# Attention with beacon keys and a gated FFN on one core: how the keys of the last three batches and the queries of the last batch are turned

## The chip, the cores and the metric

The kernel runs on one core of a Trainium2 chip, in one launch. The metric is the device time of one execution in microseconds. Before the change three runs took 399.99, 402.75 and 403.11 us, with a median of 402.75.

## The reference

Eight batches of eight heads attend, with 576 queries and 576 keys of width 64 per head, behind 16 beacon keys that every query sees; the rest is causal. The result goes through a gated FFN: 4608 tokens, width 512, hidden width 1536.

```
k_all = concatenate([beacon_k, k], axis=2)            # 16 + 576 = 592 keys
v_all = concatenate([beacon_v, v], axis=2)
scores = matmul(q, k_all.T) / sqrt(64)                # per batch and head
scores = where(key 16 + j is later than query i, -1e9, scores)
a = softmax(scores)
x = matmul(a, v_all)  -> (B * S, H * D) = (4608, 512)
out = (maximum(x @ w_gate, 0) * (x @ w_val)) @ w_out
```

## The kernel before, in words

The program is written out by a planner. Every piece of work is a `Task` with an engine, an estimated cost, the tasks that it needs and the buffers that it holds; `Plan.order` lets time run in the model, always takes the piece that can begin first (ties by priority), and the result is a fixed order of instructions for each engine. On the chip each engine goes through its order and waits on semaphores, so a cost that the planner has wrong turns into a wait and not into another order.

*Loading a batch* (`new_batch`, L497 to 676). Per batch there are a remainder each of keys and queries ("K", "Q"), four pairs of heads for keys and queries ("0" to "3", first the key pair, then the query pair) and five pieces of values. `load_pair` (L552) brings two heads of 512 tokens as float32 into a staging tile `st` (eight of them, L369). `rounded` (L508) casts it to bfloat16 in a tile `h16` (three, L371) on POOL, from batch 2 on. Then the pair is turned, so that the 64 features of two heads lie on the 128 partitions and the tokens along the columns of `kT` or `qT`:

- In batches 0 to 6 TensorE does it: `turned` (L522) issues four matmuls of the pair's four 128x128 blocks with the identity (L529) into one PSUM bank, and `evict` (L579) copies 128x512 on ScalarE or VectorE into `kT` or `qT`. The pair is loaded in runs of four tokens, 1 KB each (L563), so block j holds every fourth token, and `evict` puts the tokens in order again as it reads PSUM.
- In batch 7 (`TURN`) the DMA does it: the pair is loaded in two halves, in runs of one token of 256 bytes (L560), cast, and `dma_start_transpose` on the SP queue (L574) writes the four blocks straight to `kT` or `qT`, with no matmul and no eviction.

The remainder (64 tokens and 16 beacons of the keys, some 80 rows of the queries) goes through TensorE in all batches (`load_rest`, L610); for keys two copies bring it to `kT` (L635, L636).

*Scores* (`quad_scores`, L727). A quad is two pairs of heads, so there are two quads per batch. Each score matmul has 64 query columns as weights and up to 512 keys as the moving operand, and fills one 64x64 tile of the array; four of them (two pairs `i`, two heads `k`) go side by side. In batches 3 to 7 a quad has three steps (`STEPS2`, L337). The last holds "E", the last 64 queries against the first 512 keys, "e", the same against the next 64, and query tile 3 (256 keys):

```
for j, lo, n, b_, off in cols:        # L752
    for i in range(2):
        for k in ks:
            matmul(64x64 tile (k, i), columns off .. off + n, keys lo .. lo + n)
```

*Softmax* (`softmax`, L680). VectorE adds the mask and takes the row's lowest value in one instruction (L704, scores are negated), ScalarE writes the exponentials as bfloat16 to `pb` and their sum (L711), VectorE takes the reciprocal (L717), POOL scales (L722). From batch 1 on `pb` is transposed by DMA on the SP queue, 25 blocks of 128x128 in one instruction (L842); then TensorE makes the products with the values (L852) and the result is copied to `xT`. The last 16 queries of all heads are handled together per batch (`last`, L797, scores at L806).

*FFN* (`ffn`, L905). For ten spans of up to 512 tokens: gate and value matmuls (L913, L918), relu on ScalarE (L924), product on VectorE (L929), output matmuls (L944), eviction (L469 or L467 by the helper `copy`) and store from SP (L958). The FFN of earlier batches fills TensorE while later batches are in softmax. SP issues loads, transposes and stores in one order; loads, casts and scaling share POOL. In the first part of the plan, TensorE also runs matmuls on the identity that nothing uses (L996).

Of the kernel before, what the change touches and what calls it, by code (L numbers as in the profile page):

```python
# [35 lines left out]
TURN = (7,)  # L36
# [29 lines left out]
PACE = 38.0  # L66

# [229 lines left out]
def kernel(  # L297
# [42 lines left out]
    NB, NB0 = 25, 5  # L340

# [24 lines left out]
    kT_s = Slots(many(2, [P, NP, SK], BF16, "kT"))  # L366
# [121 lines left out]

    def heads(src, b, s0, sl):
        return src[b, :, s0:s0 + sl, :].rearrange("h s d -> s h d")  # L490
# [6 lines left out]
    def new_batch(b, prio, work):  # L497
        t = Batch()
        t.b = b
        steps = 2 * sum(len(x) for x in (STEPS2 if b > BIGSTEP else STEPS if b >= SPLIT else STEPS_AB + STEPS_CDE)) + 1  # L500
# [51 lines left out]
        def load_pair(kind, p, prio):  # L552

            src, s0 = {"k": (k, 0), "q": (q, 64 - Nb)}[kind]
            st = staged()

            def fetch(_):
                if b in TURN:
                    for i in range(2):
                        nc.sync.dma_start(st.tile.rearrange("p (n h d) -> p h n d", h=2, d=D)[:, i],  # L560
                                          src[b, 4 * (p // 2) + p % 2 + 2 * i, s0:s0 + MAIN, :].rearrange("(n p) d -> p n d", p=P))
                    return
                nc.sync.dma_start(st.tile.rearrange("p (h e) -> p h e", h=2),  # L563
                                  src[b, bass.ds(4 * (p // 2) + p % 2, 2, step=2), s0:s0 + MAIN, :].rearrange("h (p j) d -> p h (j d)", j=4))
# [3 lines left out]
            h16, ca = rounded(dst, st, P, neg_scale if kind == "q" else 1.0, prio, ld,  # L568
                              lambda to, src: [(to, src)] if b in TURN else [(
                to.rearrange("p (j h d) -> p h j d", h=2, j=4), src.rearrange("p (h j d) -> p h j d", h=2, j=4))])  # L570
            zeros = on_zeros.get(b) if kind == "q" else None
            c0 = Nb if kind == "k" else 64
            if b in TURN:
                t.rows[kind, p] = [add("DMA", (1.22, 0.177 * 4), lambda _: nc.sync.dma_start_transpose(  # L574
                    dst.tile[:, p, c0:c0 + MAIN].rearrange("p (j n) -> p j n", j=4), h16.tile), (ca, zeros), (h16, dst), prio[0] - TURN_FIRST)]
# [7 lines left out]
            t.rows[kind, p] = [add(("ACT", "DVE"), {"ACT": c_act(512), "DVE": c_dve(512)}, evict, (tu, zeros), (ps, dst), prio[1])]  # L583

# [25 lines left out]
        def load_rest(kind, prio):  # L610
# [21 lines left out]
            def evict(x):  # L632
                ps3 = ps.tile.rearrange("p (a n) -> p a n", a=NP)
                if kind == "k":
                    copy(x.engine, dst.tile[:, :, Nb + MAIN:], ps3[:, :, :REST])  # L635
# [27 lines left out]
        at, held = 0, None  # L663
# [16 lines left out]
    def softmax(t, parts, ph, prio, k):  # L680
# [3 lines left out]
        def view(i, lo=0):  # L684
            n, held, off = parts[i][:3]
            if len(held) == 1:
                return held[0].tile[:, off + lo:off + n]
            at = 512 * next(j for j, x in enumerate(bank) if x is held[0].tile)
            return psum[:, at + lo:at + n]
# [7 lines left out]
        for i, (n, held, _, msk, m, on, _, scored) in enumerate(parts):  # L697
            first = []
            if m < n:
                first = [add("DVE", c_max(n - m), lambda _, i=i, n=n, m=m: nc.vector.tensor_reduce(  # L700
                    out=at(7), in_=view(i)[:, :n - m], axis=AX.X, op=ALU.min), (scored,), held, prio + 0.001 * i + 0.0005 * k, 0.25)]

            def lowest(_, i=i, n=n, m=m, msk=msk):
                nc.vector.tensor_tensor_reduce(out=view(i, n - m), in0=view(i, n - m), in1=msk, scale=1.0,  # L704
                                               scalar=at(7) if m < n else 3.0e38,
                                               op0=ALU.add, op1=ALU.min, accum_out=at(i))

            lows.append(add("DVE", c_max(m), lowest, (scored, on, *first), held, prio + 0.001 * i + 0.0005 * k, 0.25))
        for i, (n, held, _, _, _, _, a, _) in enumerate(parts):
            def exp(_, i=i, n=n, a=a):  # L710
                nc.scalar.activation(ph.tile.rearrange("p a n -> p (a n)")[:, a:a + n], view(i), AF.Exp,  # L711
                                     bias=at(i), scale=-1.0, accum_out=at(4 + i))
# [14 lines left out]
    def quad_scores(t, g, step, phs, vals, prio, after):  # L727
# [23 lines left out]
        def scores(_):  # L751
            for j, lo, n, b_, off in cols:  # L752
                for i in range(2):
                    for k in ks:
                        r = slice(64 * k, 64 * k + 64)
                        nc.tensor.matmul(banks[k][b_].tile[64 * i:64 * i + 64, off:off + n],  # L756
                                         t.q.tile[r, 2 * g + i, 64 * j:64 * j + 64],
                                         t.kT.tile[r, 2 * g + i, lo:lo + n], start=True, stop=True)
# [17 lines left out]
    def quad(t, g, vals, prio, after):  # L776
# [4 lines left out]
        if PEQ(t.b, g):  # L781
            todo = list(range(NB_AB)) if ab else [i for i in range(21) if i not in (3, 7)] if t.b < SPLIT else list(range(NB))
            on_pe = [todo[i:i + 8] for i in range(0, len(todo), 8)]
# [13 lines left out]
    def last(t, prio):  # L797
# [17 lines left out]
    def finish(t, p, vals, ph, pt_s, blocks, on_pe, outs, prio):  # L815

        pt = Hold(pt_s, len(vals) + max(1, len(on_pe)))
        if on_pe:
            tr = []
            for todo in on_pe:  # L820
                tp = Hold(first_ps if t.b == 0 else v_ps, 2)
                z = len(todo)
                runs = []
# [4 lines left out]

                def turn(_, todo=todo, tp=tp):
# [4 lines left out]
                def evict(x, runs=runs, tp=tp):  # L834
                    for i, a, n in runs:
                        copy(x.engine, pt.tile[:, a:a + n, :].rearrange("p a n -> p (a n)"), tp.tile.bitcast(BF16)[:, i * P:(i + n) * P])

                u = add("PE", 0.06 * z, turn, outs + [on_ident], (ph, tp), prio - 4)
                more = 0.07 * (len(runs) - 1)
                tr.append(add(("ACT", "DVE"), {"ACT": c_act(z * P) + more, "DVE": 0.08 + 0.0006 * z * P + more}, evict, (u,), (tp, pt), prio - 4))  # L840
# [132 lines left out]
    for b in range(B):  # L973
        batches.append(new_batch(b, {0: -20, 1: RANK1}.get(b, b * T0 - 8), b * T0 - AHEAD if b else -20))
    for b in range(B):
        for i, vals in enumerate([("AB", "CDE")] if b >= SPLIT else [("AB",), ("CDE",)]):
            for g in range(2):
                quad(batches[b], g, vals, b * T0 + (4 * g if b >= SPLIT else 4 * i + 2 * g) - (AB_FIRST if b < SPLIT and i == 0 else 0), AFTER[b][i] if b < SPLIT else PACE * (b + g / 2))
        last(batches[b], b * T0 + 8)
# [50 lines left out]
```

## Time and profile before

| what | value |
|---|---|
| runs | 399.99, 402.75, 403.11 us, median 402.75 |
| profiled execution, its own time | 399.48 us |
| its span, first to last instruction | 397.8 us |
| mean granted TensorE clock | 0.998 |
| matmul 64 x 512 of the scores (L756), its own bar | 392 ns, 128 of them |
| relu of 128 x 512 (L924) | 604 ns |
| transposes of `pb` by DMA, issue to landing | 6.4 us median, 28 of them |

A row of instructions gives the line, the engine, the operation, output and input, the shapes and the count; behind the bar stand the busy time and the mean duration in ns, then the idle time of the engine just before and what ended it. PE is TensorE's matmuls and PEld its weight loads, DVE is VectorE, ACT ScalarE, POOL GpSimd; SPq is the queue of SyncE from which DMAs are issued, and the time of such a row is that of the issue. A matmul's bar is longer than its share of the queue, because matmuls are pipelined: what counts is the distance between starts.

### The profile page before, as it was taken

The page shows a single profiled execution, that of the slowest core. Times are in us where ns is not written, and L with a number is a line of the kernel's source. Part 1 is how long each engine was busy: PE and PEld are TensorE (multiplying, and loading weights), DVE is VectorE, ACT ScalarE, POOL GpSimd, SP SyncE. Part 2 cuts the span into 40 slices and gives each one's busy share as a digit, 9 for nine tenths or more (in the row PEclk, how much of TensorE's full clock was granted, in tenths as well). Part 3 has the DMA queues.
Part 4 walks back from the last instruction along what each step waited for, and adds up shares of the span by engine and source line. Part 5 has one row for each costly group of instructions (what it writes and reads, how often), then busy time and mean ns, then how long its engine had stood idle before and what let it go on. Part 6 is the DMA issues. An engine that isn't in the chain of part 4 may idle for free.

```text
span 397.8 us, 9897 instructions
## 1 busy us (share of the span) xinstructions
PE 386.6 (97%) x3235; PEld 203.8 (51%) x3278; DVE 287.6 (72%) x1024; ACT 261.7 (66%) x820; POOL 234.2 (59%) x454
## 2 busy tenths in 40 slices
PE   6999999999999999999999999999999999999995
PEld 4667855655454545455455445444454544444543
DVE  3999899788988697879697969687758733342432
ACT  2999699868967788668877878587737721320320
POOL 6899979849977576869669848646653520000000
PEclk9999999999999999999999999999999999999999
DMA  7999989999999799989999989798979184001102
GB/s 183 233 205 226 250 154 180 214 232 256 247 209 204 197 224 221 176 227 263 189 166 298 208 146 183 164 221 184 196 138 234 25 127 145 2 0 57 50 1 93
DMA packets 184100, 68.87 MB, mean 173 GB/s; under 512 B 158384, under 2 KB 179504, under 8 KB 184048
## 3 DMA queue, kind: packets, MB, share of 16 engines
q1 hardware_dynamic: 179216, 63.46, 73.7%
q0 software_dynamic: 4752, 4.72, 7.5%
q8 instruction: 25, 0.41, 0.5%
q14 instruction: 27, 0.22, 0.2%
q10 hardware_dynamic: 80, 0.07, 0.1%
HBM read 38.54 MB, written 9.44 MB: 121 GB/s over the span
## 4 chain that ended last, share of the span: by engine, by line
PE 88%; POOL 3%; DVE 3%; DMA 2%; issue 1%; SPq 1%; ACT 0%; POOLq 0%; ACTq 0%
PE f L918 23%; PE f L944 23%; PE f L913 22%; PE f L756 7%; PE f L852 6%; PE f L529 3%; DMA st<-in_q_dram 2%; POOL xT L722 2%; DVE f L704 2%; PE f L832 1%; PE f L996 1%; PE f L875 1%; PE f L806 1%; DVE osb L469 1%; POOL h L518 1%
## 5 line engine op out<-in xcount | busy, mean ns | idle before, releaser
L722 POOL TENSOR_SCALAR pb<-pb,small 128x448 bf16<-128x448 bf16 (+8 forms) x272 | 141.5, 539 | 70.5 <-DVE small L717 69.8
L711 ACT ACTIVATE pb<-f,small 128x320 bf16<-128x320 f32 (+8 forms) x272 | 143.9, 553 | 22.6 <-DVE small L704 17.7
L704 DVE CUSTOM_DVE_ANT_0 f<-f,mask 128x576 f32<-128x576 f32 (+8 forms) x288 | 133.7, 515 | 14.3 <-PE f L756 9.1
L918 PE MATMUL f<-xT,wv_r 128*128 128x512 bf16 (+3 forms) x467 | 107.3, 358 | 0.7
L913 PE MATMUL f<-xT,wg_r 128*128 128x512 bf16 (+3 forms) x468 | 105.4, 357 | 0.6
L929 DVE TENSOR_TENSOR hT<-g,f 128x512 bf16<-128x512 f32 (+3 forms) x120 | 75.4, 631 | 37.3 <-PE f L918 32.1
L944 PE MATMUL f<-wo_r,hT 128*128 128x512 bf16 (+3 forms) x438 | 99.6, 374 | 1.3 <-issue 0.5
L924 ACT ACTIVATE g<-f 128x512 f32<-128x512 f32 (+3 forms) x120 | 66.3, 562 | 50.9 <-PE f L913 44.2
L913 PEld LDWEIGHTS <-wg_r 128*128 128x128 bf16 x480 | 45.3, 98 | 43.7 <-issue 1.2
L918 PEld LDWEIGHTS <-wv_r 128*128 128x128 bf16 x480 | 43.4, 98 | 44.5 <-issue 5.2
L944 PEld LDWEIGHTS <-hT 128*128 128x128 bf16 (+2 forms) x456 | 42.1, 100 | 46.3 <-issue 2.1
L711 ACT ACTIVATION_READ_ACCUMULATOR pb<-f,small 128x1 f32 x272 | 60.9, 224 | 0.0
L518 POOL TENSOR_SCALAR h<-st 128x512 bf16<-128x512 f32 (+1 forms) x93 | 49.0, 541 | 11.0 <-DMA st<-in_q_dram 6.9
L469 DVE COPY osb<-f 128x512 f32<-128x512 f32 (+2 forms) x32 | 21.7, 682 | 28.1 <-PE f L944 27.7
L704 DVE DVE_READ_ACCUMULATOR2_ANT small<- 128x1 f32 x296 | 41.6, 141 | 0.0
L467 ACT CAST xT<-f 128x240 bf16<-128x240 f32 (+2 forms) x56 | 21.2, 385 | 30.7 <-PE f L852 29.5
L756 PE MATMUL f<-kT,qT 64*64 64x512 bf16 (+7 forms) x640 | 34.4, 295 | 0.1
L717 DVE RECIPROCAL small<-small 128x1 f32<-128x1 f32 (+3 forms) x136 | 20.9, 161 | 13.5 <-ACT pb L711 9.8
L529 PE MATMUL f<-ident,h 128*128 128x128 bf16 (+1 forms) x288 | 26.8, 222 | 1.6 <-POOL h L518 1.4
L529 PEld LDWEIGHTS <-h 128*128 128x128 bf16 (+1 forms) x288 | 20.0, 101 | 14.6 <-POOL h L518 4.0
L852 PE MATMUL f<-pTb,v 128*64 128x320 bf16 (+3 forms) x488 | 26.7, 253 | 0.0
L471 POOL TENSOR_SCALAR v<-st 128x512 bf16<-128x512 f32 (+1 forms) x38 | 23.2, 617 | 4.0 <-DMA st<-in_v_dram 4.0
(61 smaller groups left out, 217.5 us busy)
## 6 DMA issues: line engine op xcount, KB each, us to landing
out_dram<-osb SPq DMA_DIRECT2D x34, 256.0 KB, 2.4
st<-in_k_dram SPq DMA_DIRECT2D x28, 256.0 KB, 5.0
st<-in_q_dram SPq DMA_DIRECT2D x28, 256.0 KB, 5.1
st<-in_v_dram SPq DMA_DIRECT2D x24, 256.0 KB, 5.6
st<-in_k_dram SPq DMA_DIRECT2D x16, 128.0 KB, 4.2
st<-in_q_dram SPq DMA_DIRECT2D x16, 128.0 KB, 3.1
st<-in_v_dram SPq DMA_DIRECT2D x8, 224.0 KB, 5.2
wg_r<-in_moe_w_gate_dram POOLq DMA_DIRECT2D x3, 512.0 KB, 7.3
```

Source lines behind the costliest of these rows:

```text
L518: (nc.gpsimd if x.engine == "POOL" else nc.vector).tensor_scalar(to, src, by, 1.0, ALU.mult, ALU.mult)
L529: nc.tensor.matmul(to, h16.tile[:rows, a * P:(a + 1) * P], ident[:rows, :rows], start=True, stop=True)
L704: nc.vector.tensor_tensor_reduce(out=view(i, n - m), in0=view(i, n - m), in1=msk, scale=1.0, scalar=at(7) if m < n else 3.0e38, op0=ALU.ad ...
L711: nc.scalar.activation(ph.tile.rearrange("p a n -> p (a n)")[:, a:a + n], view(i), AF.Exp, bias=at(i), scale=-1.0, accum_out=at(4 + i))
L722: nc.gpsimd.tensor_scalar(one, one, at(8 + i), 1.0, ALU.mult, ALU.mult)
L756: nc.tensor.matmul(banks[k][b_].tile[64 * i:64 * i + 64, off:off + n], t.q.tile[r, 2 * g + i, 64 * j:64 * j + 64], t.kT.tile[r, 2 * g + i, ...
L852: nc.tensor.matmul(ps.tile[64 * hh:64 * hh + 64, d0:d0 + w], t.v.tile[:rows, c, D * h:D * h + D], rhs(64 * hh), start=(c == 0), stop=(c == ...
L913: nc.tensor.matmul(psg.tile[:, :mt], wg_r[:, ki, nf * P:(nf + 1) * P], xT[:, ki, m0:m0 + mt], start=(ki == 0), stop=(ki == KM - 1))
L918: nc.tensor.matmul(psv.tile[:, :mt], wv_r[:, ki, nf * P:(nf + 1) * P], xT[:, ki, m0:m0 + mt], start=(ki == 0), stop=(ki == KM - 1))
L924: r = add("ACT", c_act(mt), lambda _, psg=psg, g=g: nc.scalar.activation(g.tile[:, :mt], psg.tile[:, :mt], AF.Relu), (a,), (psg, g), -1000 ...
L929: hid.append(add("DVE", c_dve(mt), lambda _, psv=psv, g=g, nf=nf: nc.vector.tensor_mul(hT[nf].tile[:, :mt], g.tile[:, :mt], psv.tile[:, :m ...
L944: nc.tensor.matmul(ps[c].tile[64 * c:64 * c + rows, :w], hT[nf].tile[:, t0:t0 + rows], wo_r[:, nf, w * c:w * c + w], start=(nf == 0), stop ...
```

## The change

Keys of batches 5, 6 and 7 (`KTURN`) are turned by DMA, from pairs that are loaded in the 1-KB runs of four tokens; queries are turned by TensorE in all batches (`QTURN` is empty). Since a 1-KB run leaves every fourth token in a block, the keys of these batches lie in `kT` in four runs: run j holds the keys j, j + 4, j + 8, ... The runs are 160 columns apart (12 of padding and 148 keys), in tiles of 640 columns for all batches. What follows from that in batches 5 to 7 (`t.runs`):

- a score matmul reads the first columns of each of the four runs; "E" becomes two matmuls, of 3 x 144 and of 80 columns, that stand one behind the other for each tile (`keys`), because its 512 columns in PSUM do not end with a run;
- the scores in PSUM are in the order of the runs; the mask is read at every fourth column to match (`in_order(msk)`), and the exponentials are written at every fourth column of `pb`, so that from there on all is as before;
- the eviction of the key remainder is eight copies instead of two;
- `last` makes its scores run by run, 148 columns each.

New code that is not reached: `QUADS = 9` is above every batch, so `turned_pair` is not called; `PQUADS = 0` leaves the turning of probabilities as it was; the new lists (`LOADS`, `STEPS_AT`, `RANKS`, `LASTS`, `LAZIES`) hold the values that stood there.

```diff
-TURN = (7,)
+QUADS = 9
+KTURN = (5, 6, 7)
+QTURN = ()
+PQUADS = 0
...
+    RUN = 4
+    KW, KPAD = SK // RUN, 12
...
-    kT_s = Slots(many(2, [P, NP, SK], BF16, "kT"))
+    kT_s = Slots(many(2, [P, NP, RUN * (KPAD + KW)], BF16, "kT"))
...
+    def by_run(x):
+        return x.rearrange("p (j m) -> p j m", j=RUN)
+    def key_runs(x):
+        return by_run(x)[:, :, KPAD:]
+    def in_order(x):
+        return x.rearrange("p (m j) -> p j m", j=RUN)
...
+        t.runs = b in KTURN
...
-                if b in TURN:
+                if kind == 'q' and b in QTURN:
...
-            ld = add("DMA", (1.0, TURN_LOAD) if b in TURN else (0.5, 0.87), fetch, (held,), (st,), prio[0])
+            ld = add("DMA", (1.0, TURN_LOAD) if kind == "q" and b in QTURN else (0.5, 0.87), fetch, (held,), (st,), prio[0])
...
-            if b in TURN:
-                t.rows[kind, p] = [add("DMA", (1.22, 0.177 * 4), lambda _: nc.sync.dma_start_transpose(
-                    dst.tile[:, p, c0:c0 + MAIN].rearrange("p (j n) -> p j n", j=4), h16.tile), (ca, zeros), (h16, dst), prio[0] - TURN_FIRST)]
+            if b in (KTURN if kind == "k" else QTURN):
+                to = (lambda: key_runs(dst.tile[:, p])[:, :, Nb // RUN:(Nb + MAIN) // RUN]) if kind == "k" else (
+                    lambda: dst.tile[:, p, c0:c0 + MAIN].rearrange("p (j n) -> p j n", j=4))
+                t.rows[kind, p] = [add("DMA", (1.22, 0.177 * 4), lambda _: nc.sync.dma_start_transpose(to(), h16.tile), (ca, zeros), (h16, dst), prio[0] - TURN_FIRST)]
                 return
...
+                if kind == "k" and t.runs:
+                    for a in range(NP):
+                        for lo, n, at in ((Nb + MAIN, REST, 0), (0, Nb, REST)):
+                            copy(x.engine, key_runs(dst.tile[:, a])[:, :, lo // RUN:(lo + n) // RUN],
+                                 ps3[:, a, at:at + n].rearrange("p (m j) -> p j m", j=RUN))
+                    return
...
-                nc.vector.tensor_tensor_reduce(out=view(i, n - m), in0=view(i, n - m), in1=msk, scale=1.0,
+                own, against = view(i, n - m), msk
+                if t.runs:
+                    own, against = by_run(own) if m == n else view(i)[:, :, 512 // RUN:], in_order(msk)
+                nc.vector.tensor_tensor_reduce(out=own, in0=own, in1=against, scale=1.0,
...
-                nc.scalar.activation(ph.tile.rearrange("p a n -> p (a n)")[:, a:a + n], view(i), AF.Exp,
+                to, x = ph.tile.rearrange("p a n -> p (a n)")[:, a:a + n], view(i)
+                if t.runs:
+                    to, x = in_order(to), by_run(x) if whole[i][0] != SK else x
+                nc.scalar.activation(to, x, AF.Exp,
...
-                        nc.tensor.matmul(banks[k][b_].tile[64 * i:64 * i + 64, off:off + n],
-                                         t.q.tile[r, 2 * g + i, 64 * j:64 * j + 64],
-                                         t.kT.tile[r, 2 * g + i, lo:lo + n], start=True, stop=True)
+                        keys = [(off, n, t.kT.tile[r, 2 * g + i, lo:lo + n])]
+                        if t.runs:
+                            runs = key_runs(t.kT.tile[r, 2 * g + i])
+                            w = 64 * (j + 1) // RUN
+                            keys = [(off, n, runs[:, :, :w])] if j < TILES else [(0, 3 * w, runs[:, :3, :w]), (3 * w, 512 - 3 * w, runs[:, 3, :512 - 3 * w])] if lo == 0 else [
+                                (off, n, runs[:, 3, w - n:w])]
+                        for at, w, x in keys:
+                            nc.tensor.matmul(banks[k][b_].tile[64 * i:64 * i + 64, at:at + w],
+                                             t.q.tile[r, 2 * g + i, 64 * j:64 * j + 64], x, start=True, stop=True)
...
-            for bank, a, n in ((sc[0], 0, 512), (sc[1], 512, SK - 512)):
+            for bank, at, a, n in ((sc[0], 0, 0, 512), (sc[1], 0, 512, SK - 512)) if not t.runs else [(sc[j // 2], 256 * (j % 2), (KPAD + KW) * j + KPAD, KW) for j in range(RUN)]:
                 for pp in range(NP):
-                    nc.tensor.matmul(bank.tile[32 * pp:32 * pp + 32, :n], t.q.tile[:, pp, S + Nb - TAIL:],
+                    nc.tensor.matmul(bank.tile[32 * pp:32 * pp + 32, at:at + n], t.q.tile[:, pp, S + Nb - TAIL:],
```

More of the change, by code (lines that the diff above doesn't have):

```diff
@@ L35 @@
 ON_PE = 2
-TURN = (7,)
+QUADS = 9
+TLAZY = 0.0
+KTURN = (5, 6, 7)
+QTURN = ()
+PQUADS = 0
 TURN_FIRST = 100
@@ L661, in load_v @@
                                  (ld,), (st, t.v), prio[1])
-        at, held = 0, None
+        at, held, waiting = 0, None, []
         for what in ORDER0 if b == 0 else "KQ0011v2233vvvv":
@@ L819, in finish @@
             tr = []
+            quads = PQUADS and vals != ("F",)
             for todo in on_pe:
-                tp = Hold(first_ps if t.b == 0 else v_ps, 2)
                 z = len(todo)
+                tps = [Hold(first_ps if t.b == 0 else v_ps, 2) for _ in range(2 if quads else 1)]
+                if quads:
+                    tps[0].next, tps[1].prev = tps[1], tps[0]
+                tp = tps[0]
                 runs = []
@@ L827, in finish, with turn_quads @@
                     runs[-1][2] += 1
+                def turn_quads(_, todo=todo, tps=tps):
+                    for i, a in enumerate(todo):
+                        for k in range(2):
+                            for c in range(2):
+                                rows, cols = slice(64 * k, 64 * k + 64), slice(64 * c, 64 * c + 64)
+                                nc.tensor.transpose(tps[k].tile.bitcast(BF16)[cols, i * 64:i * 64 + 64], ph.tile[rows, a, cols], ident[rows, rows])
                 def turn(_, todo=todo, tp=tp):
```

62 lines of the change are left out of this document (52 added, 10 removed).

## The prediction

> **What bounds the kernel now.** I read the page first (busy shares, clock, chain), then the windows over the part that the change touches, then the instructions in order of time.
>
> ```profile
> PE 386.6 (97%) x3235; PEld 203.8 (51%) x3278; DVE 287.6 (72%) x1024; ACT 261.7 (66%) x820; POOL 234.2 (59%) x454
> PEclk9999999999999999999999999999999999999999
> ...
> PE 88%; POOL 3%; DVE 3%; DMA 2%; issue 1%; SPq 1%; ACT 0%; POOLq 0%; ACTq 0%
> ```
>
> TensorE is busy 97% of the span, at nearly its full clock, and 88% of the chain that ended last is its own work. A busy TensorE row can hide gaps, since ends are modelled, so the next view is the windows; the columns are window, its length, then busy time of PE, PEld, DVE, ACT, POOL, clock, DMA share, GB/s.
>
> ```profile
> 155.00:195.00 40.00, 39.62 (x347) 19.84 (x353) 33.84 (x118) 30.87 (x98) 31.61 (x60) 1.00 1.00 217
> 195.00:235.00 40.00, 39.68 (x346) 19.80 (x350) 33.83 (x121) 30.05 (x96) 29.23 (x56) 1.00 0.95 205
> 235.00:275.00 40.00, 39.47 (x317) 18.98 (x322) 30.05 (x109) 30.77 (x103) 22.98 (x46) 1.00 0.86 179
> 275.00:315.00 40.00, 39.73 (x326) 19.05 (x331) 29.69 (x103) 26.43 (x86) 23.78 (x46) 1.00 0.84 166
> 315.00:335.00 20.00, 19.89 (x124) 9.62 (x120) 8.41 (x19) 6.20 (x17) 2.88 (x5) 1.00 0.63 121
> ```
>
> From 155 us (batch 5's first loads) to 335 us TensorE is busy 39.62 + 39.68 + 39.47 + 39.73 + 19.89 = 178.4 of 180 us; 1.6 us are left. Every other engine has 6 to 17 us free in each window of 40. So the time here is the sum of what TensorE has to do. The last attention products start at 333.56, straight after an output block:
>
> ```profile
> 320.31 8.39 SPq L842 DMA_TRANSPOSE pTb<-pb  x2
> ...
> 323.10 10.52 PE L944 MATMUL f<-wo_r,hT 128*128 128x512 bf16 x47
> 333.56 1.57 PE L852 MATMUL f<-pTb,v 128*64 128x128 bf16 x32
> 335.06 1.25 PE L913 MATMUL f<-xT,wg_r 128*128 128x512 bf16 x4
> ```
>
> What the reader sees: even at the end of attention TensorE has other work up to the moment when the last transposed probabilities are there. A change can gain here only what it takes off TensorE, and at most the 1.6 us of idle time besides; it can lose what it adds there, and any wait for which no other work is ready.
>
> **The change part by part.**
>
> *Turns on TensorE.* Keys of batches 5 and 6 leave TensorE (8 pairs), queries of batch 7 come to it (4 pairs); batch 7's keys were turned by DMA already. That is 4 pairs fewer, of 4 matmuls each. What two pairs cost is seen between their neighbours:
>
> ```profile
> 219.79 1.03 PE L913 MATMUL f<-xT,wg_r 128*128 128x512 bf16 x4
> 220.66 0.70 PE L529 MATMUL f<-ident,h 128*128 128x128 bf16 x8
> 221.19 1.03 PE L918 MATMUL f<-xT,wv_r 128*128 128x512 bf16 x4
> ```
>
> The eight start at 220.66 and the next work at 221.19, so a turn takes 0.53/8 = 0.066 us of the queue, not the 0.2 us that its own bar is long. 16 turns: 16 x 0.066 = -1.06 us, all on the path.
>
> *The wide scores.* For batches 5 to 7 the keys lie in four runs, and the 512-column score matmul (the names E) becomes two: three runs of 144 (432 columns) and 80 of the fourth. In the code the two stand next to each other inside the loop over the four 64x64 tiles. Before, this step looks like this (three narrow windows of the instructions in order of time):
>
> ```profile
> 313.51 0.41 PE L756 MATMUL f<-kT,qT 64*64 64x512 bf16 x4
> ```
>
> ```profile
> 313.51 0.44 PE L756 MATMUL f<-kT,qT 64*64 64x512 bf16 x8
> ```
>
> ```profile
> 313.78 0.28 PE L756 MATMUL f<-kT,qT 64*64 64x256 bf16 x4
> 313.99 0.32 PE L852 MATMUL f<-pTb,v 128*64 128x320 bf16 x1
> ```
>
> The first window (up to 313.53) holds four starts: four matmuls of 512 columns run beside each other in four tiles. The second window (from 313.745) finds the next four begun, and by 313.78 the third group starts. Twelve matmuls with 4 x (512 + 64 + 256) = 3328 columns are through in 313.99 - 313.51 = 0.48 us; the FFN rows above give 0.87/4 = 0.217 us for 512 columns, so one after another they would have taken 1.41 us. The overlap comes from neighbours in the queue going to different tiles. In the new order the second instruction goes to the tile that the first still uses. If the queue keeps its order, it holds up the other three tiles: each of the first three waits out 432 columns, 432/512 x 0.217 = 0.183 us, before the next tile may start. That is 3 x 0.183 = 0.55 us per step, and there is one such step per quad: 2 quads x 3 batches x 0.55 = +3.29 us. If a matmul could pass a waiting one, it would be 0; that is the other end. I take 3.29: in the rows no group starts before the one ahead of it has streamed. The Trainium skill, "TensorE: Matmul & The Clock Gate", Part 3, "The mechanism", states that matmuls start and end strictly in program order and that only weight loads are pulled ahead. By that rule the sum is the one I take; no run here shows it for two matmuls of one tile in a row. The last-query scores stay in four tiles side by side (4 groups of 148 columns for 512 + 80): nothing.
>
> *Work of VectorE and ScalarE.* Four evictions of 512 columns fewer; and the key remainder, two copies before, becomes eight in each of three batches.
>
> ```profile
> L469 DVE CAST kT<-f 128x512 bf16<-128x512 f32 x15 | 10.2, 682 | 1.8 <-PE f L529 1.8
> L467 ACT CAST kT<-f 128x512 bf16<-128x512 f32 x13 | 7.8, 601 | 9.4 <-PE f L529 9.4
> L469 DVE CAST kT<-f 128x64 bf16<-128x64 f32 x6 | 1.3, 214 | 0.0
> ```
>
> ```profile
> 242.42 0.55 DVE L469 CAST kT<-f 128x256 bf16<-128x256 f32 x2
> ```
>
> Less 4 x 0.65 = 2.6 us; more 3 x (8 x 0.214 - 0.55) = 3.5 us. Both lie on engines with 6 to 10 us free in 40, so they cost TensorE nothing as sums; but each burst of 1.7 us stands ahead of an FFN eviction that the planner thinks due after 0.6 us. Bounds 0 and 3 x 1.16 = 3.5 us; I take 0.3, near nothing, because bursts of that length (two 576-column reductions of 0.77 us, rows below) exist now and TensorE idles 1.6 us in all.
>
> *Strided softmax.* The scores come out run by run, so the mask is read and the exponentials are written at every fourth element.
>
> ```profile
> L704 DVE CUSTOM_DVE_ANT_0 f<-f,mask 128x576 f32<-128x576 f32 x32 | 23.9, 773 | 5.3 <-PE f L756 2.6 <-POOL pb L722 2.5
> ...
> L704 DVE CUSTOM_DVE_ANT_0 f<-f,mask 128x128 f32<-128x128 f32 x32 | 9.2, 325 | 0.1
> ```
>
> ```profile
> L431 DVE TENSOR_REDUCE maskf<-xT x1: 368/368/368, 3.7 to 3.7; 128x16 f32<-128x128 f32 x1
> L432 DVE TENSOR_SCALAR maskf<-maskf x1: 272/272/272, 4.1 to 4.1; 128x16 f32<-128x16 f32 x1
> ```
>
> Contiguous, VectorE takes (773 - 325)/448 = 1.0 ns per column. The one reduction that reads SBUF at a step of 16 floats (L431) takes (368 - 272)/112 = 0.86 ns per column more than a 16-column instruction: no dearer. I take 0; the upper bound is twice the price, 2880 columns x 4 = 11520 per batch x 1.0 ns = 11.5 us per batch on VectorE. For ScalarE no row writes at a step; it reads PSUM at one in the eviction above (601 ns for 512) and contiguously in the relu (604, row below), no difference, so 0 again; twice its price would be 0.83 ns (from the rows below) x 11520 = 9.6 us per batch against 9 to 14 free in 40: just hidden.
>
> ```profile
> L711 ACT ACTIVATE pb<-f,small 128x576 bf16<-128x576 f32 x32 | 23.7, 744 | 6.6 <-DVE small L704 6.4 <-DVE small L717 0.2
> L924 ACT ACTIVATE g<-f 128x512 f32<-128x512 f32 x84 | 50.1, 604 | 25.9 <-PE f L913 22.6 <-PE f L918 2.0 <-PE f L756 0.5
> L711 ACT ACTIVATE pb<-f,small 128x64 bf16<-128x64 f32 x28 | 8.9, 317 | 5.5 <-DVE small L704 2.9 <-POOL h L518 1.6 <-POOL pb L722 0.8
> ```
>
> *Queues.* SP: batch 7's 16 half loads become 8, in longer runs; 4 transposes fewer there, 4 more each in batches 5 and 6. A key that waits for its transpose holds one of three cast buffers, and SP issues in order:
>
> ```profile
> 180.00 10.64 SPq L842 DMA_TRANSPOSE pTb<-pb  x2
> ```
>
> ```profile
> 179.73 1.20 POOL L518 TENSOR_SCALAR h<-st 128x512 bf16<-128x512 f32 x2
> ...
> 181.48 1.78 POOL L518 TENSOR_SCALAR h<-st 128x512 bf16<-128x512 f32 x3
> 183.55 0.62 POOL L518 TENSOR_SCALAR h<-st 128x512 bf16<-128x512 f32 x1 [0.29 <-PE f L529]
> ```
>
> ```profile
> kT<-h SPq DMA_TRANSPOSE x4, 3.2
> ```
>
> ```profile
> 285.59 1.23 SPq L574 DMA_TRANSPOSE kT<-h  x1
> ```
>
> ```profile
> 198.62 0.63 PE L756 MATMUL f<-kT,qT 64*64 64x64 bf16 x16
> ```
>
> Batch 5's keys are cast at 175 to 184. Behind the two probability transposes SP is free at 190.64; three key transposes of 1.23 us and 3.2 us to landing bring the last key to 196.3. The batch's first scores start at 198.62, so 2.3 us are left and I take 0. That cover is thin: it stands in the rivals.
>
> *Sum.* The profiled execution took 399.48 us (span 397.8): 399.48 - 1.06 + 3.29 + 0.3 = 402.0, +0.6%. The three runs shown (399.99, 402.75, 403.11) have a mean of 401.95, 2.5 above it; with that, 404.5 us, to be held against the median of 402.75.
>
> **The rivals.** (1) *The queue does not hold the tiles up*: the split costs nothing, 399.48 - 1.06 + 0.3 = 398.7, with the 2.5 us 401.2. For it speaks that the four tiles do run beside each other; against it that no group in the rows starts before the one ahead of it has streamed. (2) *The strided mask makes VectorE the bound.* Its place is every masked reduction of batches 5 to 7. At twice the price per column VectorE has 30.05 + 11.5 = 41.6 us to do in a 40 us window, and it decides from about 10 us more per batch (10/11.5 of the contiguous 1.0 ns per column). Each of three batches is then 1.6 us over, and I let the waits that follow cost as much again: 3 x 3.2 = 9.6, so 402.0 + 9.6 + 2.5 = 414.1. Against it stands L431, no dearer at a longer step. The Trainium skill, "SBUF — State Buffer", "Door 1: The DMA port swizzle", says that SBUF is read in lines of 16 bytes and wants two hits per line for full speed; every fourth float gets one, so by that rule this rival would come about. The trace's one strided row does not agree. (3) *The key transposes come late*, the other side of my forecast by one mechanism: if one of batch 5's or 6's keys falls behind another 25-block pair of transposes (10.64 us instead of 2.3 spare), the first scores wait 8.3 us; TensorE covers what FFN work it has. It decides from 2.3 us of lateness; at 7 us uncovered: 402 + 7 + 2.5 = 411.5. Against it: the plan gives a key transpose its place in SP's order before the scores that need it, and batch 7's keys already came this way (285.59 in the row above) without TensorE idling.
>
> **How the numbers follow.** Forecast 0.55 (own range 401.5 to 408); rival 1 0.15; rival 2 0.10; rival 3 0.20. A measurement of this kernel tells about 1% from no change, 398.7 to 406.8. Of the forecast 0.38 lies within and 0.17 above; of rival 1 0.12 within and 0.03 below; rival 2 above; rival 3 0.05 within and 0.15 above. Faster 0.03, same 0.55, slower 0.42. The range 400 to 412 leaves out rival 2, the low end of rival 1 and the high end of rival 3.
>
> **What would show it.** The E step: a first instruction of 432 columns, starts 0.18 us apart, the whole step 1.0 instead of 0.48 us, six times; no such spacing means rival 1. L529 with 208 matmuls of 128x128 (224 now, less those not recorded). L704 at 576 columns still near 773 ns, L711 near 744; 1.3 us there means rival 2. PE idle in the windows from 155 to 335 still about 2 us; more, with scores waiting for a kT transpose, means rival 3. The forecast is wrong if TensorE's idle time there moves by more than its work does.

## The result, and the profile after

The changed kernel takes 432.95 us in the median of six runs (432.14 to 434.27); the kernel before takes 400.25 beside it (399.49 to 403.11). The ratio is 1.080, with a 95% interval of 1.076 to 1.085: some 33 us slower, where the forecast was 404.5 us with a range of 400 to 412. In what follows, ratios leave out one run each of runs 1 and 10 that was over 1.5% above the fastest of its kernel, while medians of times keep it.

The page of the changed kernel, busy time and clock:

```profile
PE 399.0 (92%) x3310; PEld 207.7 (48%) x3310; DVE 304.3 (70%) x1034; ACT 295.9 (68%) x824; POOL 234.1 (54%) x454
PEclk9989999999999999999999989999999999999999
```

TensorE fell from 97 to 92% of a longer span; ScalarE has 34 us more to do than before, VectorE 17 us more. The windows over the part that was changed (length, then PE, PEld, DVE, ACT, POOL, clock, DMA share, GB/s):

```profile
200.00:240.00 40.00, 33.94 (x284) 16.23 (x283) 31.86 (x100) 32.95 (x82) 21.29 (x43) 1.00 0.82 170
240.00:280.00 40.00, 33.57 (x256) 15.86 (x254) 26.00 (x74) 28.68 (x67) 20.39 (x39) 0.96 0.67 139
280.00:320.00 40.00, 34.65 (x267) 16.69 (x268) 29.66 (x92) 30.92 (x78) 19.52 (x38) 1.00 0.76 165
320.00:360.00 40.00, 33.97 (x267) 16.39 (x266) 27.76 (x77) 32.59 (x75) 17.88 (x33) 1.00 0.47 95
```

TensorE is busy 136.1 of these 160 us, so 24 us are idle where before nearly none were. No other engine is full either: ScalarE, the busiest after TensorE, stands at 72 to 82%. That is the picture of engines waiting for each other, not of one that is saturated. Over the whole span TensorE's idle time grew from 397.8 - 386.6 = 11.2 to 432.4 - 399.0 = 33.4 us, so 22 of the some 33 us are idle time; the rest lies in stretches that show as busy, where bars are longer than their share of the queue and the clock is 0.96 once, and is not resolved further.

What grew is the softmax. The groups of the exponentials and the masked minimum, first before (lines L711 and L704), then after (L780 and L770); behind the bar stand busy time and the mean of one in ns:

```profile
L711 ACT ACTIVATE pb<-f,small 128x320 bf16<-128x320 f32 (+8 forms) x272 | 143.9, 553 | 22.6 <-DVE small L704 17.7
L704 DVE CUSTOM_DVE_ANT_0 f<-f,mask 128x576 f32<-128x576 f32 (+8 forms) x288 | 133.7, 515 | 14.3 <-PE f L756 9.1
```

```profile
L780 ACT ACTIVATE pb<-f,small 128x448 bf16<-128x448 f32 (+8 forms) x272 | 179.8, 726 | 33.8 <-DVE small L770 18.5
L770 DVE CUSTOM_DVE_ANT_0 f<-f,mask 128x64 f32<-128x64 f32 (+7 forms) x180 | 83.9, 511 | 8.3 <-PE f L832 5.2
L770 DVE CUSTOM_DVE_ANT_1 f<-f,mask 128x64 f32<-128x64 f32 (+8 forms) x108 | 72.9, 742 | 4.0 <-PE f L832 3.9
```

The same 272 exponentials take 726 instead of 553 ns in the mean, 272 x 0.173 = 47 us more as a sum of durations; neighbours overlap, so their busy time grew by less, 179.8 - 143.9 = 36 us. The masked minimum is busy 83.9 + 72.9 - 133.7 = 23 us more, and all of that lies in the 108 instructions of a second form (ANT_1), which is new. Restricted to batches 5 to 7 (window 198 to 358 us), by shape:

```profile
L780 ACT ACTIVATE pb<-f,small 128x576 bf16<-128x576 f32 x12 | 17.6, 1539 | 9.6 <-DVE small L770 7.0 <-POOL v L482 1.8 <-POOL pb L791 0.8
L770 DVE CUSTOM_DVE_ANT_1 f<-f,mask 128x576 f32<-128x576 f32 x12 | 14.0, 1210 | 0.0
L780 ACT ACTIVATE pb<-f,small 128x64 bf16<-128x64 f32 x12 | 4.8, 406 | 3.9 <-DVE small L770 2.9 <-issue 0.9
L770 DVE CUSTOM_DVE_ANT_1 f<-f,mask 128x64 f32<-128x64 f32 x12 | 2.8, 273 | 3.9 <-PE f L832 3.9
```

Per column that is (1539 - 406)/512 = 2.21 ns on ScalarE, where it was 0.83, and (1210 - 273)/512 = 1.83 ns on VectorE, where it was 1.0. How this reaches TensorE is seen in the instructions in order of time, around the last wide score step (rows of two engines out of one view):

```profile
346.49 0.38 PE L832 MATMUL f<-kT,qT 64*64 64x432 bf16 x2 [0.35 <-ACT g L1016]
...
347.06 1.42 ACT L780 ACTIVATE pb<-f,small 128x512 bf16<-128x512 f32 x1
...
348.23 1.44 ACT L780 ACTIVATE pb<-f,small 128x512 bf16<-128x512 f32 x1
...
348.53 0.56 PE L832 MATMUL f<-kT,qT 64*64 64x432 bf16 x14 [1.67 <-ACT pb L780]
```

The first tile begins at 346.49. The next needs a bank of PSUM that still holds scores of the step before, until ScalarE has read them; ScalarE is in the 512-column exponentials, at 1.42 us each, and TensorE stands idle for 1.67 us in the middle of a step. While it stands, the FFN matmuls behind it in its fixed order do not run, so ScalarE and VectorE get no relu or product to do: all three idle by turns. Of all waits of TensorE (total, times, longest), this one is the largest:

```profile
PE f L832 <- ACT pb L780: 8.6, 11, 1.7
```

With other work that waits for the same exponentials (3.2 and 3.0 us for the last queries' scores and the attention products, 3.0 for FFN matmuls) it is some 18 us.

### The profile page after: what moved, and what is told of

It is laid out like the page before. It is cut to its first block, busy times and chain, and to the rows that moved or that the text cites. A ratio compares the mean times of both kernels' runs of the same rounds, so it can differ in the third digit from the quotient of the medians.

```text
span 432.4 us, 10003 instructions
## 1 busy us (share of the span) xinstructions
PE 399.0 (92%) x3310; PEld 207.7 (48%) x3310; DVE 304.3 (70%) x1034; ACT 295.9 (68%) x824; POOL 234.1 (54%) x454
## 5 line engine op out<-in xcount | busy, mean ns | idle before, releaser
L780 ACT ACTIVATE pb<-f,small 128x448 bf16<-128x448 f32 (+8 forms) x272 | 179.8, 726 | 33.8 <-DVE small L770 18.5
L791 POOL TENSOR_SCALAR pb<-pb,small 128x576 bf16<-128x576 bf16 (+8 forms) x272 | 141.8, 539 | 109.1 <-DVE small L786 108.0
L1036 PE MATMUL f<-wo_r,hT 128*128 128x512 bf16 (+2 forms) x456 | 101.9, 374 | 0.0
L770 DVE CUSTOM_DVE_ANT_0 f<-f,mask 128x64 f32<-128x64 f32 (+7 forms) x180 | 83.9, 511 | 8.3 <-PE f L832 5.2
L770 DVE CUSTOM_DVE_ANT_1 f<-f,mask 128x64 f32<-128x64 f32 (+8 forms) x108 | 72.9, 742 | 4.0 <-PE f L832 3.9
L780 ACT ACTIVATION_READ_ACCUMULATOR pb<-f,small 128x1 f32 x272 | 66.1, 243 | 0.0
L832 PE MATMUL f<-kT,qT 64*64 64x64 bf16 (+9 forms) x664 | 38.8, 294 | 9.6 <-ACT pb L780 8.6
L786 DVE RECIPROCAL small<-small 128x2 f32<-128x2 f32 (+3 forms) x136 | 20.8, 161 | 38.0 <-ACT pb L780 32.6
L770 DVE DVE_READ_ACCUMULATOR2_ANT small<- 128x1 f32 x296 | 42.2, 143 | 0.0
L480 DVE COPY osb<-f 128x512 f32<-128x512 f32 (+2 forms) x29 | 19.6, 681 | 21.5 <-PE f L1036 21.3
L832 PEld LDWEIGHTS <-qT 64*64 64x64 bf16 x664 | 16.3, 107 | 35.3 <-issue 31.2
```

Of the source, the lines that this page charges most:

```text
L770: nc.vector.tensor_tensor_reduce(out=own, in0=own, in1=against, scale=1.0, scalar=at(7) if m < n else 3.0e38, op0=ALU.add, op1=ALU.min, ac ...
L780: nc.scalar.activation(to, x, AF.Exp, bias=at(i), scale=-1.0, accum_out=at(4 + i))
L791: nc.gpsimd.tensor_scalar(one, one, at(8 + i), 1.0, ALU.mult, ALU.mult)
L832: nc.tensor.matmul(banks[k][b_].tile[64 * i:64 * i + 64, at:at + w], t.q.tile[r, 2 * g + i, 64 * j:64 * j + 64], x, start=True, stop=True)
L1036: nc.tensor.matmul(ps[c].tile[64 * c:64 * c + rows, :w], hT[nf].tile[:, t0:t0 + rows], wo_r[:, nf, w * c:w * c + w], start=(nf == 0), stop ...
```

## The experiments

Each run stands beside runs of the kernel before on the same chip; ratios are to those. The rivals were: theory W, that ScalarE's write at every fourth column costs most of the 33 us; theory M, that VectorE's mask at every fourth column does; theory Q, that key transposes come late; and for the wide scores, theory F (a busy tile holds up the queue, as the prediction had it) against theory P (others pass it).

### 1. Exponentials written contiguously (changed kernel)

```diff
-                    to, x = in_order(to), by_run(x) if whole[i][0] != SK else x
+                    x = (by_run(x) if whole[i][0] != SK else x).rearrange("p j m -> p m j")
+                    to = to.rearrange("p (m j) -> p m j", j=RUN)
```

> Only the exponentials differ from the changed kernel: ScalarE reads the scores in PSUM at a step and writes the probabilities contiguously, in the order of the keys; the result is the same. Theory W (ScalarE's write at every fourth column is the cause of most of the 32 us): the row of 576 columns falls from 1539 to about 750 ns, some 47 us of ScalarE's work in three batches go, and the time falls to 405 to 415 us; what is left is the mask. Theory M (VectorE's mask at every fourth column is the cause): the time stays above 425 us. Theory Q (late key transposes): it stays above 425 us as well, and TensorE still waits.

407.5 us, ratio 1.016 (1.008 to 1.024). The step is now in the reading of PSUM, in 12 of the 32 instructions of the first row, and costs nothing (744 ns before, when all 32 read contiguously); the mask is as in the changed kernel:

```profile
L781 ACT ACTIVATE pb<-f,small 128x576 bf16<-128x576 f32 x32 | 23.7, 744 | 10.0 <-DVE small L770 8.7 <-POOL pb L792 0.9 <-DVE small L787 0.2
L770 DVE CUSTOM_DVE_ANT_1 f<-f,mask 128x576 f32<-128x576 f32 x12 | 14.0, 1207 | 0.0
```

Some 25 of the 33 us above the kernel before are gone with this one edit. Theory W takes the larger part.

### 2. Mask read contiguously (changed kernel)

```diff
-                    own, against = by_run(own) if m == n else view(i)[:, :, 512 // RUN:], in_order(msk)
+                    own = (by_run(own) if m == n else view(i)[:, :, 512 // RUN:]).rearrange("p j m -> p m j")
+                    against = msk.rearrange("p (m j) -> p m j", j=RUN)
```

> Only the mask differs from the changed kernel: VectorE goes through the scores in PSUM at a step, in the order of the keys, and reads the mask contiguously; the result is the same. Theory W: the row of 576 columns falls from 1209 to about 775 ns, but the time falls by less than 8 us, to 425 us or more, since ScalarE stays the later of the two. Theory M: the time falls to 400 to 412 us. If the price lay in the form of the instruction with a mask of two dimensions and not in the step, the row stays near 1209 ns.

423.8 us, ratio 1.058 (1.051 to 1.065):

```profile
L771 DVE CUSTOM_DVE_ANT_0 f<-f,mask 128x576 f32<-128x576 f32 x32 | 23.9, 775 | 2.8 <-PE f L833 1.4 <-POOL pb L792 1.3
```

The row is back at 775 ns, with the scores read and written at a step in PSUM in 12 of the 32. Some 9 us are gone, a little more than the 8 that theory W allowed; theory M alone is out.

### 3. Both

Edits 1 and 2 together.

> Both edits: exponentials written contiguously and mask read contiguously, from scores that are read at a step in PSUM. Theories W and M together (the softmax is all of it): 399 to 402 us, TensorE idle about 2 us in the part that was changed. Theory Q: 408 us or more remains, with scores that wait for a key transpose.

399.6 us, ratio 0.998 (0.994 to 1.002). The softmax is all of the loss. Theory Q is out for this kernel, and the wide scores, which are still split in this run, cost nothing that shows: with the prediction's 3.29 us for them, 400.13 - 1.06 + 3.29 + 0.3 = 402.7 us, the ratio would be 1.006, outside the interval. TensorE in the windows of the prediction's first table:

```profile
155.00:195.00 40.00, 39.53 (x361) 19.85 (x367) 33.45 (x124) 30.32 (x97) 30.43 (x59) 1.00 1.02 216
195.00:235.00 40.00, 39.31 (x343) 19.45 (x349) 31.81 (x122) 31.65 (x101) 27.62 (x53) 1.00 0.94 187
235.00:275.00 40.00, 39.47 (x332) 19.26 (x337) 30.15 (x112) 30.06 (x95) 27.41 (x53) 1.00 0.98 207
275.00:315.00 40.00, 39.67 (x315) 18.78 (x319) 27.34 (x99) 29.33 (x92) 22.75 (x43) 1.00 0.91 188
315.00:335.00 20.00, 19.90 (x148) 9.81 (x148) 9.68 (x25) 8.30 (x23) 5.54 (x11) 1.00 0.57 120
```

177.9 of 180 us busy, 178.4 before. DMA's share in 235 to 315 is higher than before (0.98 and 0.91 for 0.86 and 0.84), and TensorE waits for no transpose in that stretch.

### 4. The split wide score, tile by tile (changed kernel)

```diff
-                for i in range(2):
-                    for k in ks:
...
-                        for at, w, x in keys:
-                            nc.tensor.matmul(...)
+                for part in range(2 if t.runs and j == TILES and lo == 0 else 1):
+                    for i in range(2):
+                        for k in ks:
...
+                            at, w, x = keys[part]
+                            nc.tensor.matmul(...)
```

> Only the order of the split wide score differs from the changed kernel: first the 432 columns in all four tiles, then the 80 columns in all four. Theory F (a matmul whose tile is busy holds up those behind it): the step gets 0.55 us shorter, six times, and the time falls by 2 to 4 us. Theory P (matmuls of other tiles pass it, as the starts in the trace of the changed kernel suggest): within 1 us of the changed kernel's 433 us.

434.1 us, ratio 1.084 (1.077 to 1.091), which is that of the changed kernel. The time alone settles little, since TensorE idles here anyway and the interval is some 3 us to either side; run 3, where TensorE is the bound, and the trace of the changed kernel settle it for theory P. The kernel's order is 432, 80, 432, 80, ... columns. Its instructions in a window up to 212.99, in order of time and then by shape, and in a second window up to 265.48:

```profile
212.80 0.39 PE L832 MATMUL f<-kT,qT 64*64 64x432 bf16 x4
```

```profile
L832 PE MATMUL f<-kT,qT 64*64 64x432 bf16 x4 | 0.4, 368 | 0.0
```

```profile
265.24 0.42 PE L832 MATMUL f<-kT,qT 64*64 64x432 bf16 x8
```

Within 0.19 us of the first start only four have begun, all of 432 columns: the 80 columns that stand between them in the order wait for their own tile, and the next tiles pass them. Eight have begun after 0.24 us; in a strict order the eighth would start after 4 x 0.183 = 0.73 us.

### 5. The price against the step (kernel before)

```diff
+                own, against = view(i, n - m), msk
+                if t.b in {5: 2, 6: 4, 7: 8} and m == n:
+                    own, against = [y.rearrange("p (m j) -> p j m", j={5: 2, 6: 4, 7: 8}[t.b]) for y in (own, against)]
...
+                if t.b in {5: 2, 6: 4, 7: 8}:
+                    to, x = [y.rearrange("p (m j) -> p j m", j={5: 2, 6: 4, 7: 8}[t.b]) for y in (to, x)]
```

> The kernel before, where only the order in which the softmax goes through its columns differs: in batch 5 at a step of 2 columns, in batch 6 of 4, in batch 7 of 8, for the mask with its scores and for the exponentials read and written; the result is the same. It gives the price per column against the step. If ScalarE pays whenever two writes beside each other no longer follow on each other, step 2 (4 bytes) costs as much as step 4: about 1500 ns for 576 columns in all three batches. If a line of 16 bytes decides, step 2 and 4 are cheaper than step 8. For the mask (4 bytes each) the line gives near 775 ns at step 2 and 1200 ns at steps 4 and 8.

442.0 us in a single run. Rows by shape, in three windows: batch 5 (step 2), batch 6 (step 4), batch 7 (step 8):

```profile
L717 ACT ACTIVATE pb<-f,small 128x576 bf16<-128x576 f32 x4 | 3.6, 909 | 1.5 <-DVE small L707 1.3 <-POOL pb L728 0.2
L707 DVE CUSTOM_DVE_ANT_1 f<-f,mask 128x576 f32<-128x576 f32 x4 | 2.9, 777 | 0.0
L717 ACT ACTIVATE pb<-f,small 128x64 bf16<-128x64 f32 x4 | 1.3, 334 | 0.4 <-POOL pb L728 0.3
```

```profile
L717 ACT ACTIVATE pb<-f,small 128x576 bf16<-128x576 f32 x4 | 5.9, 1535 | 3.8 <-DVE small L707 3.8
L707 DVE CUSTOM_DVE_ANT_1 f<-f,mask 128x576 f32<-128x576 f32 x4 | 4.6, 1194 | 0.0
L717 ACT ACTIVATE pb<-f,small 128x64 bf16<-128x64 f32 x4 | 1.6, 406 | 0.5 <-POOL pb L728 0.4
```

```profile
L717 ACT ACTIVATE pb<-f,small 128x576 bf16<-128x576 f32 x4 | 10.8, 2937 | 3.0 <-DVE small L707 1.5 <-POOL h L518 1.4
L707 DVE CUSTOM_DVE_ANT_1 f<-f,mask 128x576 f32<-128x576 f32 x4 | 4.7, 1198 | 0.0
L717 ACT ACTIVATE pb<-f,small 128x64 bf16<-128x64 f32 x4 | 2.4, 605 | 0.7 <-POOL pb L728 0.4 <-issue 0.3
```

ScalarE's write takes (909 - 334)/512 = 1.12 ns per column at step 2, 2.21 at step 4 and 4.55 at step 8. The first guess in the expectation was wrong. The second had the order right, but 16 bytes are no threshold here: the price doubles with the step, and per 16 bytes that the write passes over (4, 2, 1 columns) it is 4.5, 4.4 and 4.55 ns. The mask came out as expected: as cheap at step 2 as contiguously (777 ns), and at steps 4 and 8 equally dear (1194, 1198). So it pays from the step on at which two columns no longer share 16 bytes, and no more beyond it, as far as these three steps show.

### 6. Strided writes alone (kernel before)

The second half of the edit above, with step 4 in batches 5 to 7.

> The kernel before, with the exponentials of batches 5 to 7 alone read and written at every fourth column; no key runs, no new transposes, mask as before. Theory W: about 47 us more of ScalarE's work, and a time of 418 to 426 us, as the changed kernel had it with its mask mended. If the loss needed the key transposes and the new loads as well (theory Q), the time stays below 410 us.

419.4 us, ratio 1.042 (1.036 to 1.048), within what theory W gave: 17.6 us are lost without key runs, new loads or new transposes. It is less than in run 2, which has the same writes in the changed kernel at 1.058 (1.051 to 1.065). The same strided writes so cost some 6 us more in the changed kernel; no run shows why.

### 7. The planner told of the prices (changed kernel)

```diff
-            lows.append(add("DVE", c_max(m), lowest, ...
+            lows.append(add("DVE", c_max(m) + (0.00078 * m if t.runs else 0.0), lowest, ...
-            sums.append(add("ACT", c_exp(n), exp, ...
+            sums.append(add("ACT", c_exp(n) + (0.00138 * n if t.runs else 0.0), exp, ...
```

> The changed kernel, with the planner told the measured prices of its strided softmax (0.00138 us more per column of the exponentials, 0.00078 us more per column of the mask); the work is the same. If the loss is that TensorE stands behind waits in an order made for cheaper work, a new order wins back most of it: 405 to 415 us. If ScalarE and VectorE simply have too much to do in the three batches, 425 to 433 us.

447.7 us, ratio 1.113 (1.108 to 1.119): worse than either expectation. The new order does not win anything back. In its trace TensorE now waits in few, long stretches, and its granted clock falls to 0.946 in the mean, where the changed kernel has 0.992:

```profile
PE f L944 <- DMA pTb<-pb: 24.7, 6, 10.0
...
PE f L550 <- POOL h L539: 9.0, 4, 5.0
```

That is 24.7 us in six waits for transposed probabilities. That the plan places the attention later and then has no FFN work left to cover it is argued from this, not shown. Telling the planner the two prices is not enough; how much of the 33 us another order could save stays open.

### 8. A mask of two dimensions without the step (kernel before)

The mask in rows of 64 columns, 80 apart, in all batches: `mask[:, 9 - n // 64:, :64]` in place of `mask[:, 512 + 64 - n:]`, and the scores viewed as rows of 64.

> The kernel before, with the mask kept in rows of 64 columns that lie 80 columns apart, so that its pattern has two dimensions but follows on itself within a row. If the form of the instruction with a two-dimensional mask costs, the row of 576 columns takes about 1200 ns; if the step of four floats costs, it stays near 775 ns.

```profile
L705 DVE CUSTOM_DVE_ANT_1 f<-f,mask 128x576 f32<-128x576 f32 x32 | 23.9, 772 | 5.1 <-PE f L757 2.5 <-POOL pb L723 2.4
```

772 ns, and 402.0 us in a single run: the step costs, the second form of the instruction doesn't.

### 9 to 12. More turned by DMA, with a clean softmax

All four start from run 3. `KTURN = (3, 4, 5, 6, 7)`:

> The kernel with both softmax edits (contiguous writes, contiguous mask), and the keys of batches 3 to 7 turned by DMA instead of 5 to 7. Against the kernel before TensorE has 12 pairs of turns fewer, 12 x 0.265 = 3.2 us. If TensorE's work alone sets the time: 396.5 to 397.5 us where the kernel before takes 400. If the transposes on SP and the DMA engines have no room for 8 more of them (theory Q), 400 us or more, with scores or casts that wait.

419.6 us, ratio 1.047 (1.042 to 1.052). `KTURN = (1, ..., 7)`:

> The same with the keys of batches 1 to 7 turned by DMA: 20 pairs fewer, 20 x 0.265 = 5.3 us. TensorE's work alone: about 394.7 us where the kernel before takes 400; in the first part of the plan idle time is filled with matmuls that nothing uses, so part of the gain of batches 1 and 2 may go into those. Theory Q: above 400 us, and more than with batches 3 to 7.

413.7 us, ratio 1.031 (1.026 to 1.036). `QTURN = (7,)`, that is, one thing more by DMA than in run 3:

> The kernel with both softmax edits, keys of batches 5 to 7 turned by DMA, and the queries of batch 7 by DMA as before the change: 8 pairs of turns fewer than before, 2.1 us, but the loads of batch 7's queries in runs of 256 bytes and four transposes more. TensorE's work alone: about 398 us where the kernel before takes 400, 1 us below the kernel with both softmax edits. If the queues matter there: no gain, or a loss of 1 us or more.

415.2 us, ratio 1.035 (1.030 to 1.040). And the keys of batches 1 to 7 with `FILLED = 40.0`:

> The kernel with both softmax edits and the keys of batches 1 to 7 turned by DMA, which ran 211 of the matmuls that nothing uses where the kernel before runs 88; now the planner may place them up to its time 40 instead of 160, so that those after about 30 us go. If they stood in the way, 123 x 0.11 = 13.5 us go from 413.7: about 400 us, level with the kernel before, and below it by as much as the 20 pairs of turns bring. If TensorE would have idled in those places anyway, the time stays above 408 us.

414.2 us, ratio 1.031 (1.025 to 1.037). The matmuls that nothing uses are 87 in the trace (211 in run 10, 88 in the kernel before), and TensorE idles in their place: it is busy 32.0 of 40 us where run 10 had 38.7, at a granted clock of 0.83 for 1.00:

```profile
80.00:120.00 40.00, 31.98 (x292) 16.58 (x295) 27.15 (x105) 22.10 (x71) 26.00 (x49) 0.83 0.98 217
```

Fewer turns on TensorE, and 12 to 18 us lost each time, all on theory Q's side; but run 10, with more turned by DMA, lost less than run 9, against its expectation. In the `QTURN` run the idle time lies elsewhere than in run 12, at the end of attention. The waits of TensorE (total, times, longest) and of POOL, and the place:

```profile
PE f L946 <- DMA pTb<-pb: 12.6, 3, 8.6
```

```profile
POOL h L539 <- DMA kT<-h: 11.6, 2, 11.1
```

```profile
332.65 0.88 PE L946 MATMUL f<-pTb,v 128*64 128x128 bf16 x16 [1.83 <-DMA pTb<-pb]
342.13 1.55 PE L946 MATMUL f<-pTb,v 128*64 128x128 bf16 x16 [8.60 <-DMA pTb<-pb]
345.82 1.54 PE L946 MATMUL f<-pTb,v 128*64 128x128 bf16 x16 [2.14 <-DMA pTb<-pb]
```

12.6 us of idle time, all in the last three products of batch 7: the FFN work that stands before them at 323 to 333 us in the kernel before is used up. The clock adds to it: the same 16 products take 0.88 us before the wait of 8.60 us and 1.55 behind it, and over these 40 us the granted clock is 0.79:

```profile
320.00:360.00 40.00, 27.43 (x185) 12.96 (x184) 17.25 (x55) 13.65 (x43) 9.90 (x20) 0.79 0.52 109
```

POOL waited 11.1 us at a stretch for a cast buffer that a key transpose held. That this wait is what made the last batch late is argued from the trace and not shown: a fourth cast buffer, which could show it, was not tried. So no version here beats the kernel before; run 3 is level with it.

## Why the prediction was wrong, step by step

- *Bound.* Right: before, TensorE's work is the time, and what isn't covered is lost one for one. That the changed part could gain hardly anything was right too.
- *Turns on TensorE, -1.06 us.* Consistent: run 3, which has these turns and a clean softmax, is at 0.998 (0.994 to 1.002). -1.06 of 400 is 0.997; zero is not excluded. The trace of the changed kernel has the 208 matmuls of 128x128 that the prediction named.
- *The wide scores, +3.29 us.* Wrong, and in a step of its own: the queue does not hold up other tiles (run 3 and the starts above); nothing of it shows in the time, as rival 1 had it. The rule of the Trainium skill that the prediction cited ("TensorE: Matmul & The Clock Gate", Part 3, "The mechanism"), of matmuls that start and end strictly in program order, does not agree with these traces where the waiting matmul and the next are in different tiles: the 80 columns of the first tile start at 213.01, behind the 432 columns of the other three at 212.81 to 212.82. Taking the rule over the open row cost 3 us, and moved the forecast the right way for a wrong reason.
- *Evictions, +0.3 us.* Nothing to be seen of it in run 3.
- *Strided softmax, 0.* This is the step that failed. It is 36 us of ScalarE's and 23 us of VectorE's busy time, and 33 us of time (runs 1 to 3: about 25 for the writes, 7 to 9 for the mask). Three errors lie in it. First, for ScalarE the prediction took a row that *reads PSUM* at a step as evidence for one that *writes SBUF* at a step; reading is free (run 1), writing is not. Where no row shows an operation, twice its price was an arbitrary end; it was 2.7 times (2.21 for 0.83 ns per column). Second, for VectorE the row was there and was read wrongly: L431 (368 ns for 128 columns at a step) was compared with a 16-column instruction of another kind. The kernel has a reduction that reads contiguously, from PSUM and to one result per row where L431 forms 16:

```profile
L700 DVE TENSOR_REDUCE small<-f x8: 681/692/693, 39.0 to 303.5; 128x1 f32<-128x512 f32 x8
```

  At 1.0 ns per column its fixed part is 692 - 512 = 180 ns. If L431 has the same fixed part, which is an estimate, it paid (368 - 180)/128 = 1.5 ns per column, half as much again. Third, the cover. "9 to 14 us free in 40" was taken to hide work on ScalarE. But a softmax step holds PSUM banks that the next score step needs, TensorE stands in a fixed order behind that, and time was lost with ScalarE at 72 to 82%.
- *Queues, 0.* Right for this change (run 3), and thin as said: with more turned by DMA, 12 to 18 us are gone (runs 9 to 12); rival 3 had allowed 7 us, and that late key transposes are the cause there is not shown.
- *Rivals and range.* Rival 2 named the mask, gave it 0.10 and 414 us; on its own the mask is worth 7 to 9 us (run 2, and run 1 against run 3). No rival had the exponentials, which are three quarters of it. The 0.58 on "same" or faster came from pricing both at 0.

## What to carry to other kernels

When a layout changes, ask of every operand separately whether it is now read or written at a step, and in which memory: here the same step was free on PSUM reads, cost 1.8 times on an SBUF mask and 2.7 times on bfloat16 writes, and moving it from the write to the read removed the larger part of the loss with one edit. Price a step from a row of the same instruction, or leave it as an unknown with a wide end. And idle time of an engine is cover only if nothing that the bound engine needs is held while the engine works.

## What the runs showed of the hardware

- ScalarE writing bfloat16 to SBUF at a step of 2, 4 or 8 columns takes 1.12, 2.21 and 4.55 ns per column, some 4.5 ns for every 16 bytes passed over; contiguously it takes 0.83 ns per column, and reading float32 from PSUM at a step adds nothing to that (744 ns for 576 columns in run 1 as before).
- VectorE reading a float32 mask from SBUF: 777 ns for 576 columns at step 2, 1194 at step 4, 1198 at step 8, 773 contiguously. The Trainium skill, "SBUF — State Buffer", "Door 1: The DMA port swizzle", has lines of 16 bytes that want two hits each. The mask agrees with the two hits. The write doesn't: at a step of 4 bfloat16 there are two hits per line, and it costs 2.7 times as much.
- Matmuls in other tiles of the array pass one that waits for its tile: four starts in the first 0.19 us, with the 80-column matmuls between them in the order not yet begun.
- TensorE's granted clock fell where TensorE had stood idle for long: in run 11 the same 16 products took 0.88 us before a wait of 8.60 us and 1.55 us behind it, with a clock of 0.79 over these 40 us.
